# Loading one group's output weights last in a streaming attention decode kernel

## Chip, cores, metric

One core of one Trainium2 chip. The metric is device time in microseconds (us) of one launch. Before the change it is 666.4 us (median; all runs between 666.25 and 666.71 in the first measurement).

## The reference

One decode step: layer norm, grouped-query attention over a cache of 65,536 keys for 8 KV heads (4 query heads each), and beside it a small GELU MLP; all is added to `x`.

```python
q = (xn @ wq)                                  # 32 heads of 128
scores = einsum("bhqd,bhkd->bhqk", q, k) * Dh**-0.5
o = einsum("bhqk,bhkd->bhqd", softmax(scores), v)
out = x + o.reshape(B, Sq, 32 * 128) @ wo + (gelu(xn @ w1 + b1) @ w2 + b2)
```

K and V are 268 MB together in bf16. `wo` has 4096 rows of 512 values; a row is 1 KB, one head's rows are 128 KB.

## The kernel before

Engines are named as in the profile: PE multiplies matrices, DVE does elementwise vector work, ACT the exponentials, and SP issues the loads. K(n) and V(n) are chunk n of the K and V cache.

The kernel walks through 32 chunks of K and 32 of V, 4 MB each, with four chunk buffers. A chunk of K is transposed on PE, copied back, multiplied with q; a chunk of V is multiplied with the softmax weights ("PV"), 128 matmuls that add up in `pO`. Chunk 31 (`L`) is the last; its V comes in five pieces so that PE can follow the transfer closely. The wo of the last six heads comes in one load in the middle of the stream.

```python
LASTP = (64, 32, 16, 8, 8)                     # tiles of the last V chunk per load
# ... in the issue loop, for V of the last chunk:
t0 = 0
for i, n in enumerate(LASTP):
    sch.dma(SP, lambda ...: sp.dma_start(out=slot[b][:, t0:t0 + n, :], in_=src[:, t0:t0 + n, :]),
            lsem[i], writes=[f"last{i}"] + ...)
    t0 += n
# ...
def dma_wo_end():                              # issued behind V(16), at 347 us
    sch.dma(SP, lambda: sp.dma_start(
        out=wo_end[:, :, :], in_=A_wo[(H - HT) * DH:, :].rearrange("(h p) n -> p h n", p=128)),
        sem_wo, writes=["wo_end"])
```

The end of the program, after the last V chunk but one:

```python
heads(GL, 0, HPG, oT_bf, "oT")                 # the last group's output from its first 3 chunks
for i in range(len(LASTP)):
    pv(L, range(cuts[i], cuts[i + 1]), f"last{i}")
    if i == 0:
        wo_part(wo_end, "wo_end", oT_bf, "oT", HPG, HW)   # 16 matmuls: these 3 chunks times wo
    if i == 1:
        ...                                    # finT (all earlier heads' output), transposed into pR
oL_bf = pO * coef                              # DVE: the last chunk's part
for j in range(HPG):
    for kt in range(KT):
        pR[kt] += oL_bf[:, j] x wo_end[:, HW + j, kt]     # 16 matmuls
fin_bf = pR                                    # DVE cast, then the store
```

## Time and profile before

The kernel streams. The page's DMA lines (40 equal slices of the span; share of 16 DMA engines in tenths, then GB/s), queue 1 (packets, MB, share of the engines' time) and the HBM total:

```profile
DMA  9999999999999999999999999999999999999995
GB/s 379 417 433 434 417 434 429 428 436 426 430 428 432 430 426 434 428 430 425 428 440 426 422 419 437 427 428 438 427 430 432 428 430 426 436 424 433 422 427 226
q1 hardware_dynamic: 14844, 280.51, 98.9%
HBM read 280.50 MB, written 0.00 MB: 422 GB/s over the span
```

Only the last slice is not full. So the place to look at is the end. The chain that ended last, in order of time (start us, length us, what):

```profile
621.90 28.98 DMA kv<-in_A_v_cache_dram
650.88 0.05 issue
650.92 3.57 PE pO L562 x128
...
660.89 0.03 issue
660.91 0.39 PE pO L562 x8
661.30 0.02 issue
661.32 0.17 DVE oL_bf L821
661.50 0.04 issue
661.54 0.62 PE pss L825 x14
662.16 0.02 issue
662.19 0.29 DVE fin_bf L831
```

The last eight PV matmuls stand apart because they wait for the last V piece. After it come one multiply, 16 wo matmuls (the chain counts 14 of them) and the cast. The store is issued at 662.51 and the span ends at 664.57.

The trace also has each load's semaphore updates, one for each of the 16 DMA engines that carry it. The Trainium skill ("DMA: Bandwidth & Descriptors", section "Why a DMA increments its semaphore by 16 and not by 1") says that these engines finish independently and that only the full 16 mean that all has landed. The trace agrees with the first of these, and shows how far apart they are. The updates of the last V piece, in us:

```
655.98 655.99 656.06 656.15 656.25 656.28 657.29 657.34 657.56 658.67 658.96 658.97 659.03 659.17 659.28 660.87
```

One engine is 1.59 us behind the fifteenth, and 4.9 behind the first. It sets each landing at the end. (The updates do not name their engine. That it is the same one each time is inferred: from 600 us on, every load of the stream has such a last update, 1.58 to 1.62 us behind the fifteenth.) Below, "stream end" is the last update of the last input load, here 660.87. From there to the cast at 662.19 are 1.32 us; call that the *gap*.

| kernel before | us |
|---|---|
| time, median | 666.4 |
| V(30) landed | 650.88 |
| stream end (last V piece landed) | 660.87 |
| gap, stream end to cast | 1.32 |
| 768 KB of wo on the lagging engine (379.29 to 381.53) | 2.24 |

### The profile page before, as it was taken

To read this page: it belongs to the slowest core of one execution; us is meant where nothing else is said; L and a number is where in the kernel's file an instruction comes from. 1 tells how busy PE (TensorE), PEld (TensorE's weight loads), DVE (VectorE), ACT (ScalarE), POOL (GpSimd) and SP (SyncE) were. 2 spreads that over 40 slices of the span, in tenths; PEclk is the share of its full clock that TensorE was granted. 3 is DMA by queue.
4 is the path that set the end of the run, shared out by engine and by line. 5 is a ranking of instruction groups with operands and counts; after the bars stand their busy time and mean duration, and the time that the engine had idled before them with its cause. 6 is when DMAs were issued, how large, how long until landed. Compare 5 with 4: busy or idle time off the path is not lost.

```text
span 664.6 us, 27512 instructions
## 1 busy us (share of the span) xinstructions
PE 556.8 (84%) x12862; PEld 527.2 (79%) x12862; DVE 273.7 (41%) x628; ACT 244.5 (37%) x469; POOL 2.3 (0%) x13
## 2 busy tenths in 40 slices
PE   2799769999887899878889878898778898877896
PEld 2789669998877888877789777898777798877795
DVE  0445224454433444444344433345433354433441
ACT  1354134444422344432344423344323344422340
POOL 1000000000000000000000000000000000000000
PEclk9887578887766787766788767888767887766785
DMA  9999999999999999999999999999999999999995
GB/s 379 417 433 434 417 434 429 428 436 426 430 428 432 430 426 434 428 430 425 428 440 426 422 419 437 427 428 438 427 430 432 428 430 426 436 424 433 422 427 226
DMA packets 14868, 280.82 MB, mean 423 GB/s; under 512 B 1658, under 2 KB 5756, under 8 KB 6140
## 3 DMA queue, kind: packets, MB, share of 16 engines
q1 hardware_dynamic: 14844, 280.51, 98.9%
q8 instruction: 14, 0.23, 0.1%
q14 instruction: 10, 0.08, 0.0%
HBM read 280.50 MB, written 0.00 MB: 422 GB/s over the span
## 4 chain that ended last, share of the span: by engine, by line
DMA 58%; PE 38%; issue 2%; ACT 1%; DVE 0%
DMA kv<-in_A_k_cache_dram 54%; PE pst L487 26%; PE pss L507 4%; DMA kv<-in_A_v_cache_dram 4%; PE pO L562 3%; PE pA L528 1%; PE pA L538 1%; PE pA L580 1%; PE pA L595 1%; ACT kt_ring L497 0%; PE pA L622 0%; ACT P_bf L548 0%; ACT L548 0%; ACT L472 0%; PE pA L665 0%
## 5 line engine op out<-in xcount | busy, mean ns | idle before, releaser
L487 PE MATMUL pst<-ident_bf,kv 128*128 128x128 bf16 x4096 | 312.3, 245 | 87.2 <-DMA kv<-in_A_k_cache_dram 85.5
L487 PEld LDWEIGHTS pst<-ident_bf,kv 128*128 128x128 bf16 x4096 | 284.3, 112 | 105.7 <-DMA kv<-in_A_k_cache_dram 74.4
L497 ACT ACTIVATE kt_ring<-pst 128x1024 bf16<-128x1024 bf16 x192 | 197.8, 1031 | 395.2 <-PE pst L487 392.6
L495 DVE COPY kt_ring<-pst 128x1024 bf16<-128x1024 bf16 x320 | 211.6, 688 | 215.6 <-PE pst L487 214.7
L562 PE MATMUL pO<-P_bf,kv 128*128 128x4 bf16 x4096 | 120.9, 166 | 12.0 <-issue 10.1
L562 PEld LDWEIGHTS pO<-P_bf,kv 128*128 128x128 bf16 x4096 | 114.2, 101 | 13.1 <-issue 11.0
L507 PE MATMUL pss<-q_cur,kt_ring 128*128 128x4 bf16 x4096 | 121.5, 165 | 1.6 <-issue 1.1
L507 PEld LDWEIGHTS pss<-q_cur,kt_ring 128*128 128x128 bf16 x4096 | 116.3, 98 | 1.8 <-issue 1.2
L515 DVE TENSOR_REDUCE pmax<-pss 128x4 f32<-128x512 f32 x32 | 22.1, 692 | 103.9 <-PE pss L507 103.9
L548 ACT ACTIVATE P_bf<-pss,negm 128x128 bf16<-128x128 f32 x128 | 50.8, 551 | 7.6 <-DVE negm L541 7.6
L548 ACT ACTIVATION_READ_ACCUMULATOR P_bf<-pss,negm 128x1 f32 x128 | 36.0, 282 | 0.0
L571 DVE COPY o_all<-pO 128x4 f32<-128x4 f32 x31 | 5.0, 162 | 38.6 <-PE pO L562 38.6
L528 PE MATMUL pA<-ident_f,pmax 128*4 128x128 f32 x64 | 16.0, 344 | 0.3 <-DVE finT L700 0.3
L538 PE MATMUL pA<-diag,ones_f 4*128 4x4 f32 x64 | 12.4, 261 | 0.3 <-DVE finT L700 0.3
L538 PEld LDWEIGHTS pA<-diag,ones_f 4*128 4x128 f32 x64 | 9.6, 187 | 3.6 <-DVE finT L700 0.3
L530 DVE TENSOR_REDUCE gmax<-pA 4x1 f32<-4x128 f32 x32 | 8.6, 269 | 0.7 <-PE pA L528 0.7
L532 DVE TENSOR_SCALAR diag<-ident_f,gmax 4x4 f32<-4x4 f32 x32 | 7.0, 217 | 1.1
L528 PEld LDWEIGHTS pA<-ident_f,pmax 128*4 128x4 f32 x64 | 2.9, 84 | 5.5 <-DVE kt_ring L495 4.1
L665 PE MATMUL pA<-sums_cur,ones_f 128*128 128x16 f32 x32 | 6.4, 277 | 0.0
L541 DVE TENSOR_SCALAR negm<-pA 128x4 f32<-128x4 f32 x32 | 5.1, 160 | 0.7 <-PE pA L538 0.7
L695 PE MATMUL pA<-oT_cur,wo_cur 128*128 128x1 bf16 x120 | 5.3, 166 | 0.0
L665 PEld LDWEIGHTS pA<-sums_cur,ones_f 128*128 128x128 f32 x32 | 5.2, 205 | 0.0
(75 smaller groups left out, 62.0 us busy)
## 6 DMA issues: line engine op xcount, KB each, us to landing
kv<-in_A_k_cache_dram SPq DMA_DIRECT2D x32, 4096.0 KB, 28.4
kv<-in_A_v_cache_dram SPq DMA_DIRECT2D x31, 4096.0 KB, 32.4
kv<-in_A_wq_dram SPq DMA_DIRECT2D x1, 4096.0 KB, 20.0
kv<-in_B_w_dram SPq DMA_DIRECT2D x2, 1792.0 KB, 36.3
wo_cur<-in_A_wo_dram SPq DMA_DIRECT2D x13, 256.0 KB
kv<-in_A_v_cache_dram SPq DMA_DIRECT2D x1, 2048.0 KB, 27.9
kv<-in_A_v_cache_dram SPq DMA_DIRECT2D x1, 1024.0 KB, 30.0
wo_end<-in_A_wo_dram SPq DMA_DIRECT2D x1, 768.0 KB, 34.1
```

Source lines behind the costliest of these rows:

```text
L487: lambda tb=tb, at=at, b=b, tt=s * TPB + t: pe.transpose(pst[tb][:, at * 128:(at + 1) * 128], slot[b][:, tt, :], ident_bf[:, :]),
L495: e, fn = DVE, lambda tb=tb, dst=dst: dve.tensor_copy(out=dst, in_=pst[tb][:, :])
L497: e, fn = ACT, lambda tb=tb, dst=dst: act.activation(out=dst, in_=pst[tb][:, :], func=ACTF.Copy)
L507: lambda k=k, kb=kb, at=at, t=t: pe.matmul(pss[k][:, at:at + HPG], lhsT=kt_ring[:, kb * BCOL + t * 128:kb * BCOL + (t + 1) * 128], rhs=q_c ...
L515: lambda k=k: dve.tensor_reduce(out=pmax[:, :], in_=pss[k][:, 0:CW].rearrange("p (t j) -> p j t", j=HPG), axis=AX.X, op=ALU.max),
L528: sch.op(PE, lambda: pe.matmul(pA[0:HPG, PA_ST:PA_ST + 128], lhsT=pmax[:, 0:HPG], rhs=ident_f[:, :], start=True, stop=True), reads=["pmax" ...
L530: sch.op(DVE, lambda: dve.tensor_reduce(out=gmax4[:, :], in_=pA[0:HPG, PA_ST:PA_ST + 128], axis=AX.X, op=ALU.max), reads=["pA"], writes=[" ...
L532: sch.op(DVE, lambda: dve.tensor_scalar(out=diag4[:, :], in0=ident_f[0:HPG, 0:HPG], scalar1=gmax4[0:HPG, 0:1], scalar2=None, op0=ALU.mult) ...
L538: sch.op(PE, lambda: pe.matmul(pA[:, PA_SB:PA_SB + HPG], lhsT=ones_f[0:HPG, 0:128], rhs=diag4[0:HPG, 0:HPG], start=True, stop=True), reads ...
L548: lambda k=k, u=u, j=j, src=src: act.activation(out=P_v[k][:, :, j], in_=src[:, :, j], func=ACTF.Exp, bias=negm[:, u * HPG + j:u * HPG + j ...
L562: lambda k=k, b=b, t=t: pe.matmul(pO[:, 0:HPG], lhsT=slot[b][:, t, :], rhs=P_v[k][:, t, :], start=t == 0, stop=t == TPD - 1),
L665: sch.op(PE, lambda: pe.matmul(pA[:, PA_SUM:PA_SUM + GW], lhsT=ones_f[:, :], rhs=sums_cur[:, :], start=True, stop=True), reads=["ones_f", ...
```

## The change

Half a megabyte of wo, the last group's four heads, is taken out of the mid-stream load and put behind the last V piece: three heads, then one. V then lands earlier, and what lands last needs little work. So that all of wo is needed only at the very end, the four chunks' outputs of the last group are added up before the product with wo: 16 of the 32 wo matmuls fall away, one DVE operation more stands between PV and wo. V(31) comes in four pieces instead of five.

```diff
-    LASTP = (64, 32, 16, 8, 8)
+    LASTP = (64, 32, 16, 16)
+    LASTH = (HPG - 1, 1)
...
                     t0 += n
+                dma_wo_last()
...
+    def dma_wo_last():
+        h0 = 0
+        for i, n in enumerate(LASTH):
+            sch.dma(SP, lambda h0=h0, n=n: sp.dma_start(
+                out=wo_end[:, HW + h0:HW + h0 + n, :],
+                in_=A_wo[(H - HPG + h0) * DH:(H - HPG + h0 + n) * DH, :].rearrange(...)),
+                hsem[i], writes=[f"wo_last{i}"])
+            h0 += n
...
-    heads(GL, 0, HPG, oT_bf, "oT")
+    o_sum[last group] *= rden[last group]            # DVE
+    pR = finT, transposed                            # moved here from behind V piece 1
     for i in range(len(LASTP)):
         pv(L, range(cuts[i], cuts[i + 1]), f"last{i}")
-        if i == 0:
-            wo_part(wo_end, "wo_end", oT_bf, "oT", HPG, HW)
-    oL_bf = pO * coef
-    for j in range(HPG): ...                         # 16 matmuls, wait for wo_end
+    o_c = pO * coef
+    oL_bf = o_c + o_sum
+    for i in range(len(LASTH)): ...                  # 12 matmuls wait for wo_last0, 4 for wo_last1
```

(The lines on `o_sum`, `pR`, `o_c` and `oL_bf` are shortened to what they compute.)

More of the change, by code (lines that the diff above doesn't have):

```diff
@@ L331, in bass_parallel_sum__gqa_block_cached__dense_activation_gelu__decode_kernel @@
     o_sum = nc.alloc_sbuf_tensor("o_sum", [128, H], F32)
-    oT_bf = nc.alloc_sbuf_tensor("oT_bf", [128, HPG], BF)
     oT_cur = nc.alloc_sbuf_tensor("oT_cur", [128, HW], BF)
@@ L359, in bass_parallel_sum__gqa_block_cached__dense_activation_gelu__decode_kernel @@
     sem_wo = sch.dsem("dwo")
+    hsem = [sch.dsem(f"hsem{i}") for i in range(len(LASTH))]
     sem_out = sch.dsem("dout")
@@ L443, in dma_wo_end @@
         sch.dma(SP, lambda: sp.dma_start(
-            out=wo_end[:, :, :], in_=A_wo[(H - HT) * DH:, :].rearrange("(h p) n -> p h n", p=128)),
+            out=wo_end[:, 0:HW, :],
+            in_=A_wo[(H - HT) * DH:(H - HPG) * DH, :].rearrange("(h p) n -> p h n", p=128)),
             sem_wo, writes=["wo_end"])
+    def dma_wo_last():
[3 more added lines that the diff above has]
+                out=wo_end[:, HW + h0:HW + h0 + n, :],
+                in_=A_wo[(H - HPG + h0) * DH:(H - HPG + h0 + n) * DH, :].rearrange("(h p) n -> p h n", p=128)),
+                hsem[i], writes=[f"wo_last{i}"])
+            h0 += n
     after_chunk[("K", 0)] = [dma_small, dma_wq]
@@ L807, in bass_parallel_sum__gqa_block_cached__dense_activation_gelu__decode_kernel @@
     weigh_3(GL, CPG - 1)
-    heads(GL, 0, HPG, oT_bf, "oT")
+    sch.op(DVE, lambda: dve.tensor_tensor(out=o_sum[:, GL * HPG:], in0=o_sum[:, GL * HPG:],
+                                          in1=rden[:, GL * HPG:], op=ALU.mult),
+           reads=[f"o_sum{GL}", f"rden{GL}"], writes=[f"o_sum{GL}"])
     pR = pss[(L - 1) % 2]
+    for kt in range(KT):
+        sch.op(PE, lambda kt=kt: pe.matmul(pR[32 * kt:32 * kt + 1, 0:128], lhsT=finT[:, kt:kt + 1],
+                                           rhs=ident_f[:, :], start=True, stop=False),
+               reads=["finT", "ident_f"], writes=[f"pss{(L - 1) % 2}"], publish=kt == KT - 1)
     cuts = [sum(LASTP[:i]) for i in range(len(LASTP) + 1)]
@@ L813, in bass_parallel_sum__gqa_block_cached__dense_activation_gelu__decode_kernel @@
         pv(L, range(cuts[i], cuts[i + 1]), f"last{i}")
-        if i == 0:
-            wo_part(wo_end, "wo_end", oT_bf, "oT", HPG, HW)
-        if i == 1:
-            for kt in range(KT):
-                sch.op(PE, lambda kt=kt: pe.matmul(pR[32 * kt:32 * kt + 1, 0:128], lhsT=finT[:, kt:kt + 1],
-                                                   rhs=ident_f[:, :], start=True, stop=False),
-                       reads=["finT", "ident_f"], writes=[f"pss{(L - 1) % 2}"], publish=kt == KT - 1)
-    sch.op(DVE, lambda: dve.tensor_tensor(out=oL_bf[:, :], in0=pO[:, 0:HPG], in1=coef[:, L * HPG:], op=ALU.mult),
-           reads=["pO", "coefL"], writes=["oL"])
-    for j in range(HPG):
-        for kt in range(KT):
-            sch.op(PE, lambda j=j, kt=kt: pe.matmul(
-                pR[32 * kt:32 * kt + 1, 0:128], lhsT=oL_bf[:, j:j + 1],
-                rhs=wo_end[:, HW + j, kt * 128:(kt + 1) * 128], start=False, stop=j == HPG - 1),
-                reads=["oL", "wo_end"], writes=[f"pss{(L - 1) % 2}"],
-                publish=j == HPG - 1 and kt == KT - 1)
+    sch.op(DVE, lambda: dve.tensor_tensor(out=o_c[:, L * HPG:], in0=pO[:, 0:HPG], in1=coef[:, L * HPG:],
+                                          op=ALU.mult),
+           reads=["pO", "coefL"], writes=["o_cL"])
+    sch.op(DVE, lambda: dve.tensor_tensor(out=oL_bf[:, :], in0=o_c[:, L * HPG:], in1=o_sum[:, GL * HPG:],
+                                          op=ALU.add),
+           reads=["o_cL", f"o_sum{GL}"], writes=["oL"])
+    hcuts = [sum(LASTH[:i]) for i in range(len(LASTH) + 1)]
+    for i in range(len(LASTH)):
+        for j in range(hcuts[i], hcuts[i + 1]):
+            for kt in range(KT):
+                sch.op(PE, lambda j=j, kt=kt: pe.matmul(
+                    pR[32 * kt:32 * kt + 1, 0:128], lhsT=oL_bf[:, j:j + 1],
+                    rhs=wo_end[:, HW + j, kt * 128:(kt + 1) * 128], start=False, stop=j == HPG - 1),
+                    reads=["oL", f"wo_last{i}"], writes=[f"pss{(L - 1) % 2}"],
+                    publish=j == HPG - 1 and kt == KT - 1)
     NR = 32 * (KT - 1) + 1
```

## The prediction

> **What bounds the kernel now.** It streams. The page's DMA row is 9 in all slices but the last; queue 1 is busy 98.9% of 16 engines' span; HBM reads run at 422 GB/s. Less PE or DVE work inside the stream is worth nothing; only the stream and what follows its last byte count.
>
> **The tail.** The Trainium skill (DMA: Bandwidth & Descriptors, "Why a DMA increments its semaphore by 16 and not by 1") says that a DMA's 16 engines finish independently and each adds one. The trace agrees: the increments of the last V piece spread from 655.98 to 660.87 us; fifteen engines are done at 659.28, one lags alone by 1.6 us. That lag is the same on every load back to 616 us, so this engine always has queued work and its queue sets the end. Its landings: V(30) 650.88, the pieces of V(31) 655.81, 658.26, 659.55, 660.22, 660.87. In the timeline and the chain PE follows: the last eight PV matmuls start at 660.91 (0.39 us), oL multiply 661.32 (0.16), 16 wo matmuls 661.54 to 662.16, cast 662.19 (0.29), store issue 662.51, end of span 664.57. So 1.3 us lie between the last landing and the cast; 2.4 us from the cast on are fixed.
>
> **What changes.**
> - Bytes: the same. 512 KB of wo leave the load at 347 us and go behind V(31). On the lagging engine the 768 KB load took 2.23 us and the 256 KB ones 0.72, so 512 KB are about 1.48 us (estimate, linear): all of V lands about 1.5 us earlier, the last V piece at about 659.4, three heads at 660.5, the last head at 660.9, as late as the last V piece did.
> - Work after the last byte: before, 8 PV, a multiply, 16 matmuls: 1.3 us. After: four matmuls of one head, about 0.38 us with the 0.04 us wake-up (one of these lasts 0.31).
> - The V side must be ready: 659.4 + 0.04, 16 PV 0.61, two DVE operations of 0.16 with 0.05 between, so oL at about 660.45; twelve matmuls for three heads, 0.24 after 660.53, are issued before the last head lands. It just fits, with 0.1 to 0.2 us of slack.
> - PE loses 16 wo matmuls and their finT addition (0.43 us); the ident transposes move before V(31); one DVE multiply and one DMA are added. All inside waits for DMA, worth about 0.
>
> **Sum.** The cast starts at about 661.3 instead of 662.19: 0.85 us less, 0.13%. If the V side ended last, it would be about 0.7. Predicted 665.55 us, 8 in 10 between 664.9 and 666.2. Faster by over 2%: 0.005; within 2%: 0.99; slower by over 2%: 0.005.
>
> **What would show it.** V(30)'s last landing about 1.5 us earlier against the end; the last wo landing within 0.2 us of 660.9; cast at about 661.3; the chain ending wo DMA, four matmuls, cast, store; a wo_end load at 347 us of a third of its size; PE idle before V(31)'s pieces.
>
> **What would make it wrong.** (1) The lag differs between executions, or drains otherwise: the end moves by as much as the gain. (2) The wo matmuls wake later than 0.04 us after the landing. (3) PE at its 0.50 clock falls behind: its slack before V(30) is 0.83 us, and if K(31)'s stage doesn't start earlier too, V's earlier landing is partly lost. (4) Small wo transfers at the drained end are slower than in mid-stream. (5) Execution noise, 0.46 us over three runs, is half the gain.

## The result, and the profile after

The kernel after takes 665.27 us (665.20 to 665.36, 4 runs), against 666.42 us (666.25 to 666.71, 4 runs) before: 1.15 us less. The ratio is 0.9983, with a 95% interval of 0.9969 to 0.9997. The prediction was 665.55, within 664.9 to 666.2. That range also holds a gain of only 0.2 us, so it is the landings, not the time, that must confirm the account.

The DMA lines of the page after. The stream is as full as before, and the mean rate is the same within 0.3%:

```profile
DMA  9999999999999999999999999999999999999996
q1 hardware_dynamic: 14732, 280.51, 99.1%
HBM read 280.50 MB, written 0.00 MB: 423 GB/s over the span
```

The chain that ended last now runs over the wo load, not over V:

```profile
628.37 31.80 DMA wo_end<-in_A_wo_dram
660.17 0.14 issue
660.30 0.62 PE pss L842 x16
660.92 0.02 issue
660.95 0.29 DVE fin_bf L848
```

The chain shows 16 matmuls behind the load of three heads. Single records show two groups in it: the last weight loads start at 660.547, 0.05 us after the last head's landing at 660.50, and the last four matmuls run from 660.574 on, 0.31 us each.

The timeline of the end (start us, busy us, engine, line, what, in brackets the idle time before and its releaser):

```profile
657.82 0.59 PE L574 MATMUL pO<-P_bf,kv 128*128 128x4 bf16 x16 [0.22 <-DMA kv<-in_A_v_cache_dram]
659.11 0.58 PE L574 MATMUL pO<-P_bf,kv 128*128 128x4 bf16 x16 [0.69 <-DMA kv<-in_A_v_cache_dram]
659.73 0.16 DVE L832 TENSOR_TENSOR o_c<-pO,coef 128x4 f32<-128x4 f32 x1 [5.23 <-PE pO L574]
659.93 0.16 DVE L835 TENSOR_TENSOR oL_bf<-o_c,o_sum 128x4 bf16<-128x4 f32 x1
660.30 0.60 PE L842 MATMUL pss<-wo_end,oL_bf 128*1 128x128 bf16 x16 [0.61 <-DMA wo_end<-in_A_wo_dram]
660.95 0.29 DVE L848 CAST fin_bf<-pss 97x128 bf16<-97x128 f32 x1 [0.85 <-PE pss L842]
```

PE is idle before each of the last two V pieces and again before wo: there it waits for data. `oL_bf` is done at 660.09, the three heads land at 660.17: the V side is ready 0.08 us before it is needed.

On the lagging engine, the landings give the account of the 1.24 us by which the cast moved (662.19 to 660.95):

- The gap fell from 1.32 to 0.45 us: 0.87.
- The stream end moved from 660.87 to 660.50: 0.37. Of this 0.21 arose between 461 and 471 us, where both kernels do the same: one 4 MB chunk took 10.35 us before and 10.14 after. Whether that is chance is tested below.

### The profile page after: what moved, and what is told of

The parts are those of the page before. It is cut to its first block, busy times and chain, and to the rows that moved or that the text cites. A ratio compares the mean times of both kernels' runs of the same rounds, so it can differ in the third digit from the quotient of the medians.

```text
span 663.3 us, 27482 instructions
## 1 busy us (share of the span) xinstructions
PE 560.4 (84%) x12846; PEld 529.3 (80%) x12846; DVE 274.0 (41%) x628; ACT 244.5 (37%) x469; POOL 2.3 (0%) x13
## 4 chain that ended last, share of the span: by engine, by line
DMA 62%; PE 34%; issue 2%; ACT 1%; SPq 0%; DVE 0%
DMA kv<-in_A_k_cache_dram 57%; PE pst L499 25%; DMA wo_end<-in_A_wo_dram 5%; PE pss L519 4%; PE pO L574 2%; PE pA L540 1%; PE pA L550 1%; PE pA L592 1%; PE pA L607 1%; ACT kt_ring L509 0%; PE pA L634 0%; SPq L406 0%; ACT P_bf L560 0%; ACT L560 0%; ACT L484 0%
## 5 line engine op out<-in xcount | busy, mean ns | idle before, releaser
L499 PE MATMUL pst<-ident_bf,kv 128*128 128x128 bf16 x4096 | 315.8, 246 | 84.2 <-DMA kv<-in_A_k_cache_dram 82.6
L499 PEld LDWEIGHTS pst<-ident_bf,kv 128*128 128x128 bf16 x4096 | 287.3, 112 | 103.5 <-DMA kv<-in_A_k_cache_dram 71.4
L592 PE MATMUL pA<-xnT_bf,kv 128*128 128x1 bf16 x128 | 3.5, 164 | 1.8 <-DVE xnT_bf L487 1.8
```

The costliest lines, as they stand in the source:

```text
L499: lambda tb=tb, at=at, b=b, tt=s * TPB + t: pe.transpose(pst[tb][:, at * 128:(at + 1) * 128], slot[b][:, tt, :], ident_bf[:, :]),
L592: lambda h=h, kt=kt: pe.matmul(pA[:, PA_Q + h:PA_Q + h + 1], lhsT=wq_sb[:, kt, h * DH:(h + 1) * DH], rhs=xnT_bf[:, kt:kt + 1], start=kt == ...
```

## The experiments

Theory A, the prediction's: the stream ends when it ends; only the gap shrank, since four matmuls follow the last byte instead of PV, a multiply and 16 matmuls. Rival B: the gain is PE's saved work (16 matmuls and a DVE addition). Rival C: the stream itself became cheaper, by fewer V pieces or by wo at another place.

### e1: the new arithmetic alone, wo early

```diff
 (against after)
-            out=wo_end[:, 0:HW, :], in_=A_wo[(H - HT) * DH:(H - HPG) * DH, :]...
+            out=wo_end[:, :, :], in_=A_wo[(H - HT) * DH:, :]...
-                dma_wo_last()
-                reads=["oL", f"wo_last{i}"]
+                reads=["oL", "wo_end"]
```

> The new arithmetic and PE order alone; all of wo loaded in mid-stream as before, V(31) in the new four pieces. Theory A (only what follows the last byte counts): last V piece lands at the stream's end, about 660.8 us, then 16 PV 0.61, two DVE operations, 16 wo matmuls 0.62: 1.7 us from landing to cast against 1.32 before, so about 0.3 to 0.4 us slower than before, 1.5 slower than after. Theory B (less work on PE is the gain): as fast as after or at least 0.4 us faster than before. Theory C (a cheaper stream from fewer V pieces): stream end about 0.3 us earlier than before.

Measured: 666.77 us (666.55 to 666.81, 4 runs), before in the same rounds 666.37 (7 runs): 0.40 slower; the ratio is 1.0007 with an interval of 0.9991 to 1.0024, so by timing alone it is not separated from before. The stream ends at 660.67, and the trace shows what follows:

```profile
660.72 0.58 PE L573 MATMUL pO<-P_bf,kv 128*128 128x4 bf16 x16 [0.68 <-DMA kv<-in_A_v_cache_dram]
661.34 0.16 DVE L831 TENSOR_TENSOR o_c<-pO,coef 128x4 f32<-128x4 f32 x1 [5.20 <-PE pO L573]
661.53 0.16 DVE L834 TENSOR_TENSOR oL_bf<-o_c,o_sum 128x4 bf16<-128x4 f32 x1
661.75 0.60 PE L841 MATMUL pss<-wo_end,oL_bf 128*1 128x128 bf16 x16 [0.45 <-DVE oL_bf L834]
662.40 0.29 DVE L847 CAST fin_bf<-pss 97x128 bf16<-97x128 f32 x1 [0.70 <-PE pss L841]
```

The gap is 1.73 us, the longest chain so far, although PE has the same reduced work as in after. B falls: the saved matmuls were worth nothing, and the rewritten end, taken alone, costs 0.41 us of gap. Of C, e1 decides little: C expected the stream to end 0.3 us earlier than before; it ended 0.20 earlier in this profile, and by the timings about 0.06 earlier (last table).

### e2: four heads in one load

```diff
-    LASTH = (HPG - 1, 1)
+    LASTH = (HPG,)
```

> As after, but wo of the last group is one load of four heads. Theory A: last landing as in after (660.5) or 0.02 earlier, then 0.05 wake, 16 matmuls 0.62 instead of four 0.36: cast about 0.25 us later than in after, so 0.25 us slower than after and still 0.9 faster than before. Theory B: the split is worth nothing, same as after within 0.05 us.

Measured: 665.74 us (665.52 to 665.85, 4 runs), 0.63 less than before in the same rounds (ratio 0.9992, 0.9976 to 1.0009, which includes 1, so the trace has to carry it). The stream ends at 660.58; the gap is 0.78 us, 0.33 longer than in after:

```profile
660.00 0.16 DVE L835 TENSOR_TENSOR oL_bf<-o_c,o_sum 128x4 bf16<-128x4 f32 x1
660.71 0.59 PE L842 MATMUL pss<-wo_end,oL_bf 128*1 128x128 bf16 x16 [0.95 <-DMA wo_end<-in_A_wo_dram]
661.36 0.29 DVE L848 CAST fin_bf<-pss 97x128 bf16<-97x128 f32 x1 [1.20 <-PE pss L842]
```

`oL_bf` is ready here half a microsecond before PE may start. The split is worth the 0.33 us of gap, as A has it (0.25 expected): with it, twelve of the matmuls start before the last head is there.

### e3: the same loads, the last V piece behind wo

```diff
                 for i, n in enumerate(LASTP):
+                    if i == len(LASTP) - 1:
+                        dma_wo_last()
                     sch.dma(SP, ...)
-                dma_wo_last()
```

> As after, same loads and same arithmetic, but the two wo loads are issued before the last V piece, not behind it. Theory A: stream end as in after (660.5); the last V piece lands last and 1.7 us lie between it and the cast, against 0.45: 1.2 us slower than after, about as slow as before (666.4). Theories B and C: as fast as after, since the work and the bytes are the same.

Measured: 666.66 us (666.60 to 666.84, 4 runs), before in the same rounds 666.37; the interval of the ratio, 0.9989 to 1.0023, includes 1. It is 0.92 us over e2, which has wo last and ran in the same rounds, and 1.39 us over after's first measurement, which was on another occasion. Stream end 660.81, gap 1.73:

```profile
660.85 0.59 PE L575 MATMUL pO<-P_bf,kv 128*128 128x4 bf16 x16 [2.13 <-DMA kv<-in_A_v_cache_dram]
661.89 0.59 PE L843 MATMUL pss<-wo_end,oL_bf 128*1 128x128 bf16 x16 [0.45 <-DVE oL_bf L836]
662.54 0.29 DVE L849 CAST fin_bf<-pss 97x128 bf16<-97x128 f32 x1 [0.70 <-PE pss L843]
```

This is the cleanest test. The kernel has the bytes, the loads and the arithmetic of after; two loads have changed places with one. The whole gain is gone. So it is the order of the last loads that counts.

### e4: which DMA engine lags

```diff
+            for a, b in ((0, 120), (120, 128)):      # two loads by partitions instead of one
-                out=wo_end[:, HW + h0:HW + h0 + n, :], ...
+                out=wo_end[a:b, HW + h0:HW + h0 + n, :], ...
```

> As after, but each of the two last wo loads is split by partitions into 120 and 8, so that the trace shows which of the DMA engines take part in the part of 120 (15 of them[...]) and in the part of 8 (8 of them). If the one engine that lags by 1.4 us is not among the 15 nor the 8, the stream ends up to 1.4 us earlier and the kernel is up to 1 us faster than after (V side then ends last); if it is the one with both parts, it carries 36 rows instead of 32 and two more loads, 0.2 to 0.3 us slower than after; otherwise about 0.05 to 0.1 slower for two more loads.

Measured: 667.75 us (667.59 to 668.26, 4 runs), 1.38 us slower than before in the same rounds (ratio 1.0024, 1.0007 to 1.0040). None of the three expectations holds. The tail of the stream itself became slower: V(31)'s second piece landed 3.73 us after the first instead of 2.50, and the last input landed at 663.20.

```profile
658.12 1.01 PE L576 MATMUL pO<-P_bf,kv 128*128 128x4 bf16 x32 [1.27 <-DMA kv<-in_A_v_cache_dram]
661.59 0.59 PE L576 MATMUL pO<-P_bf,kv 128*128 128x4 bf16 x16 [1.23 <-DMA kv<-in_A_v_cache_dram]
662.89 0.63 PE L844 MATMUL pss<-wo_end,oL_bf 128*1 128x128 bf16 x16 [0.71 <-DMA wo_end<-in_A_wo_dram]
```

Single packets took longer: between 655 and 660 us a median of 61 ns for 1 KB and 244 ns for 4 KB, where after has 46 and 162. So with the split loads queued, even the V loads beside them were slower. Whether that comes from the partition counts or from having four loads in place of two was not tried.

The landings do tell something of the lagging engine. Each pair of split loads has 23 updates by engines, 15 and 8. In both pairs the last two come 1.6 us or more behind all others (663.02 and 663.20 after 661.42 in the last pair), where a V piece has one such update. This fits one lagging engine that carries a share of both parts; it is an inference, and the engine's number stays unknown. Relieving it stays untried.

### r1 and r2: both kernels again

No edit; both were run again in one set of rounds, for the 0.37 us of stream end. They were run on another chip.

> The kernel before against itself. The first profiles put the stream's end at 660.87 for before and 660.50 for after, of which 0.21 arose between 461 and 471 us, where the two kernels do the same. If that part is chance, a second profile of before has a stream end that differs from 660.87 by 0.1 to 0.3 us either way, still with 1.32 us from last landing to cast. If it is the change, this run ends at 660.87 within 0.05. Time the same as before.

> The changed kernel again. Theory A alone (the same stream, 0.87 us less from last landing to cast): 0.85 to 0.9 us less than before in the same rounds, stream end between 660.5 and 660.9. If the earlier end of the stream is an effect of the change: again 1.1 to 1.2 us less, stream end 660.50 within 0.05.

Measured: before 666.40 us (666.20 to 666.56, 5 runs), stream end 660.81, gap 1.33. After 665.44 us (665.29 to 665.61, 5 runs), stream end 660.84, gap 0.44; the other runs of before in these rounds have a median of 666.42. So this time the gain is 0.98 us, the ratio 0.9986 (0.9972 to 1.0000). The lines that make the gap of r1 (first two) and of r2:

```profile
660.86 0.38 PE L562 MATMUL pO<-P_bf,kv 128*128 128x4 bf16 x8 [0.27 <-DMA kv<-in_A_v_cache_dram]
662.13 0.29 DVE L831 CAST fin_bf<-pss 97x128 bf16<-97x128 f32 x1 [0.70 <-PE pss L825]
660.63 0.60 PE L842 MATMUL pss<-wo_end,oL_bf 128*1 128x128 bf16 x16 [0.60 <-DMA wo_end<-in_A_wo_dram]
661.28 0.29 DVE L848 CAST fin_bf<-pss 97x128 bf16<-97x128 f32 x1 [0.86 <-PE pss L842]
```

With equal gaps as at first, the two stream ends came out 0.03 us the other way round. The chunk at 461 us took 10.40 in r1 and 10.51 in r2, against 10.35 and 10.14 at first. Expecting r1 to differ by 0.1 or more was too narrow: the variation showed in after.

The record keeps a second profiled execution of r1, r2, e6 and e7 each. It repeats the gaps within about 0.02 us, but not the stream ends:

| kernel | stream end, quoted profile | stream end, second profile | gap, second profile |
|---|---|---|---|
| r1 (before) | 660.81 | 661.05 | 1.32 |
| r2 (after) | 660.84 | 660.50 | 0.43 |
| e6 | 660.58 | 660.83 | 0.71 |
| e7 | 660.81 | 660.89 | 0.43 |

In the second profiles the chunk at 461 us took 10.57 in r1 and 9.86 in r2. So executions of one kernel differ by up to 0.65 us in this chunk and 0.34 in the stream end, and the 0.21 lies inside that. That the change has no small part in it is not shown: in its three profiles, after's stream ends earlier twice.

### e6: the last two V pieces as one

```diff
-    LASTP = (64, 32, 16, 16)
+    LASTP = (64, 32, 32)
```

> As after, but the last two V pieces of 16 tiles are one of 32. Theory A with the V side just ready in time: the last V landing doesn't move (1.44 before the last wo landing), PE then has 32 PV matmuls instead of 16, 0.45 us more, so oL comes 0.4 us after the three heads have landed and the 16 wo matmuls end 0.65 us after it: from last wo landing to cast about 0.75 to 0.8 instead of 0.45, time 0.3 to 0.35 us over after. If the V side had much slack: same as after.

Measured: 665.52 us (665.41 to 665.60, 5 runs), only 0.08 over r2 in the same rounds, where 0.30 to 0.35 were expected. The profile has the mechanism as expected: three heads landed at 660.24, `oL_bf` came at 660.59, and PE started on wo only then; the gap is 0.72.

```profile
659.18 1.01 PE L574 MATMUL pO<-P_bf,kv 128*128 128x4 bf16 x32 [1.33 <-DMA kv<-in_A_v_cache_dram]
660.43 0.16 DVE L835 TENSOR_TENSOR oL_bf<-o_c,o_sum 128x4 bf16<-128x4 f32 x1
660.65 0.60 PE L842 MATMUL pss<-wo_end,oL_bf 128*1 128x128 bf16 x16 [0.45 <-DVE oL_bf L835]
661.30 0.29 DVE L848 CAST fin_bf<-pss 97x128 bf16<-97x128 f32 x1 [0.70 <-PE pss L842]
```

The 0.28 us of gap were mostly given back by a stream that ended earlier, at 660.58. One piece less gives 0.04 us of that (from V(30) to the end of V(31) 9.91 us, in r2 9.95). The rest, some 0.15 to 0.2 us, is of the size by which stream ends differ anyway, and e6's second profile does not show it: there the stream ends at 660.83, again with a gap of 0.71. Chance is the likely reading; the runs do not prove it.

### e7: five V pieces as before

```diff
-    LASTP = (64, 32, 16, 16)
+    LASTP = (64, 32, 16, 8, 8)
```

> As after, but V(31) comes in the five pieces of before (64, 32, 16, 8, 8). If the fewer pieces of the change shortened the stream (theory C), 0.05 us or more over after; theory A: one more load costs 0.02 to 0.04 us of stream, the V side is ready 0.2 us earlier and waits for wo, so the same as after within 0.1 us.

Measured: 665.47 us (665.40 to 665.53, 5 runs), the same as r2 (665.44). V(31) takes 10.00 us from V(30)'s landing, 0.05 more than in r2. The V side is ready 0.24 us earlier than in r2 (`oL_bf` from 660.02 instead of 660.26) and waits:

```profile
660.02 0.16 DVE L835 TENSOR_TENSOR oL_bf<-o_c,o_sum 128x4 bf16<-128x4 f32 x1
660.61 0.60 PE L842 MATMUL pss<-wo_end,oL_bf 128*1 128x128 bf16 x16 [0.82 <-DMA wo_end<-in_A_wo_dram]
```

Gap 0.45. An earlier V side buys nothing more.

### All together

Time minus span is 1.78 to 1.88 us in the profiled runs where both are known to 0.01 us (1.84 is taken here), and span minus cast 2.38, so the median time minus 4.22 minus the gap estimates a kernel's typical stream end, to about 0.1 us.

| kernel | wo of the last group | median us | stream end in its profile | gap | typical stream end, estimate |
|---|---|---|---|---|---|
| before | mid-stream | 666.42 | 660.87 | 1.32 | 660.88 |
| r1 (before) | mid-stream | 666.40 | 660.81 | 1.33 | 660.85 |
| e1 | mid-stream | 666.77 | 660.67 | 1.73 | 660.82 |
| after | last, 3 + 1 | 665.27 | 660.50 | 0.45 | 660.60 |
| r2 (after) | last, 3 + 1 | 665.44 | 660.84 | 0.44 | 660.78 |
| e2 | last, 4 | 665.74 | 660.58 | 0.78 | 660.74 |
| e3 | before the last V piece | 666.66 | 660.81 | 1.73 | 660.71 |
| e6 | last, 3 + 1 | 665.52 | 660.58 | 0.72 | 660.58 |
| e7 | last, 3 + 1 | 665.47 | 660.81 | 0.45 | 660.80 |

The gap goes from 0.44 to 1.73 and moves the time with it; the stream end stays within 0.37 us in this table. The kernels with wo at the end of the stream have a mean of 660.70 in the last column, the others 660.85. With the second profiles counted in, the stream ends themselves have the same two means, 660.70 in nine profiles and 660.85 in four. Of these 0.15 us, about 0.1 are seen in the landings of after against before: V(31) in four pieces takes 9.94 us from V(30)'s landing instead of 9.99, and the 512 KB of wo take 1.44 us at the end (1.11 and 0.33), where the same bytes made a mid-stream load longer by 1.49 (2.21 us for 768 KB in e1, 0.72 for 256 KB in r2). So C has a small share. The timings fit: over all runs of both kernels (25 of before, 9 of after) the mean gain is 1.01 us, 0.13 more than the gap gives.

## Why the prediction was right

- *The stream ends at about the same time*: right on the average, not in each profile. The prediction's own test, the last wo landing within 0.2 us of 660.9, was met once (660.84) and missed twice (660.50 in after and in r2's second profile). Before's ends are 660.87, 660.81 and 661.05. The sum took the stream end as equal; by the landings it is about 0.1 us earlier, a small term that was left out. The rest is not separated from chance.
- *Gap from 1.3 to about 0.42 us*: measured 0.45 and 0.44. The step that carries the prediction held, e3 shows it by order alone, and e1 shows that less PE work does not bring it.
- *V lands 1.5 us earlier*: V(30) 1.76 us in the first pair of profiles, 1.38 in r1 and r2 (650.82 and 649.44). Counted from the stream end, which is what was predicted, V(30) lands 11.38 us before it instead of 9.99: 1.39 earlier, and 1.41 in r1 and r2. The missing 0.1 is the cheaper loads of C.
- *The V side just fits, with 0.1 to 0.2 us of slack*: 0.08 in after. e6, with `oL_bf` 0.43 us later against the stream end than in r2, loses 0.28 us of gap; e7, with V earlier, gains none.
- *Wake-up 0.04 us after a landing*: 0.05 for the last four matmuls, 0.13 for the first matmul behind the three heads. The latter costs nothing, since the last head comes later.
- *PE keeps up at its lower clock*: it did, with 0.32 us of idle time left before V(30), where it had 0.83.
- *0.85 us in all*: 1.15 at first, 0.98 the second time. The gap gives 0.88 of both; the rest is the stream end, about 0.1 of it from cheaper loads. The first figure is larger by scatter that nobody predicted: after's runs themselves differ by 0.17 us between the two occasions.

## What to carry to other kernels

In a kernel bound by its input stream, ask of the loads not how large they are but how much work hangs on the last one, and send last what needs the least. Split that last load so that all but a little of its work is done before it is complete, and check that the side that is now earlier is ready in time: more lead than that is worth nothing. When effects are a tenth of a per cent, separate the stream's end from what follows it in the trace; timings alone would have given e6 a wrong reading.

## What the Trainium skill lacked or had wrong

- "DMA: Bandwidth & Descriptors": it says that engines finish independently, and elsewhere that two of them are usually slower, but gives no size for either. Here the 16 engines of one load were 4.8 to 5.4 us apart at the end of the runs (e4 left out), and one alone lagged 1.1 to 1.8 us behind the others; this engine sets every landing there. Nothing was found that relieves it.
- The same page, section "Specifications", has 512 B as the least size for line rate. Here a 1 KB packet took 46 ns in the median and a 32 KB packet 1216 ns, so a KB cost 46 ns in rows of wo and 38 in V: rows of 1 KB were still 21% dearer (if a row is what the page means by a transfer).
- No page read for this has what follows: with the last wo loads split into 120 and 8 partitions (e4), packets of wo and of the V loads beside them took longer, 61 ns in place of 46 per 1 KB and 244 in place of 162 per 4 KB. The cause is not settled.
- No page read for this has it: issuing a load can itself be held up. SP usually needs 0.33 to 0.44 us for one. With the V pieces and wo queued, the second wo load took 7.31 us to issue in after (434 ns the first), and both together 13.48 us in e7. It cost nothing here, since the data moved some 20 us later; with less lead it could. The two lines, of SP's timeline in after and in e7:

```profile
628.37 7.79 SPq L453 DMA_DIRECT2D wo_end<-in_A_wo_dram  x2
```

```profile
628.53 13.48 SPq L453 DMA_DIRECT2D wo_end<-in_A_wo_dram  x2
```
